# One written-out order for QKV, W1 and W2, 15 more warm-up transposes, and other staging rows for the last eight down tiles

## The chip, the cores and the metric

The kernel runs on one core of a Trainium2 chip. A core has five engines with a queue each: TensorE (PE) multiplies matrices, VectorE (DVE), ScalarE (ACT) and GpSimd (POOL) work on vectors, and SyncE (SP) issues DMAs. Each queue is worked off in order; an instruction that waits holds back everything behind it in its own queue and nothing in the others. The metric is device time in microseconds (us) of one execution; lower is better.

## The reference, cut to what matters

x has 2048 tokens of 576 channels. Two branches read the same layer-normed x, and their results are added to x.

```
xn  = layernorm(x)
out = x + A(xn) + B(xn)

A(x): qkv = layernorm-ed x @ wqkv          # 576 x 1728, 32 heads of 18
      windowed attention (8 keys, stride 2), then @ wo
B(x): h  = gelu(layernorm(x) @ w1)         # 576 x 576
      hs = shift(h) @ w2                   # four channel groups shifted by +1, -1, +2, -2 tokens
      x1 = x + hs
      x1 + gelu(layernorm(x1) @ w3) @ w4   # 576 x 4608 and 4608 x 576
```

## The kernel before

Everything is computed in single precision out of fp32r operands: each operand is split into a high part (a copy by ACT) and a low part (a subtraction by DVE), and a product is the sum of three matmuls (high x high, high x low, low x high). 576 rows are four blocks of 128 and a rest of 64; in PAIRS this gives 14 matmuls for an output tile. Tokens come in 16 tiles of 128 (t) and, transposed, in four blocks of 512 (b). Y holds the 16 token tiles in SBUF and rows of it serve as scratch in between.

The stages follow each other: QKV, W1, W2, then W3 and W4 with the attention beside them, then the output product with wo. The program is written in Python without a scheduler: the order in which the lines run is the order in each engine's queue.

**QKV** is written as a list. Each name of ORDER_Q (line 53) is a small function in T, and `for name in ORDER_Q.split(): T[name]()` runs them. The names that the prediction uses:

- x0 to x15 load a token tile, st its statistics (DVE, then a power by POOL), no its normalisation (DVE). ta copies its tail columns, tm and tt transpose main part and tail on PE into a PSUM tile of the pool psb (three of them), ch, cl, ct, cu cut the transposed tile into high and low parts (h and t on ACT, l and u on DVE).
- c0.0 to c3.2 load a column group of wqkv in three parts (two main parts, then the tail in four DMAs); wh, wl, wL, wt, wu, wU split it (h and t on ACT, l and u on DVE, L and U on POOL).
- u0.0 to u23.3 are the matmuls of 24 plain units of 14 matmuls each, in four pieces (6, 2, 4, 2); u0o copies the result out, u0s stores it to DRAM (qkvd). The pieces need, in this order: high parts and one low weight part, the other low weight part, the low part of x, the tails.
- zpad stores zeros in front of qkvd. pw does not exist before.
- From "mid" on, g6 to g15 are sums of seven products each on pairs of token tiles, fed by zg, zt, zp (a turned copy through DRAM), gp (reading it back), sx and ph, pl, pt, pu (sums and splits).
- w1m, w1t load w1, w1h and w1l split it; gz0.0 to gz0.5 load z, the turned x of a block of 512 tokens, and z0t, z0h0, z0h1 (ACT) and z0u, z0l0, z0l1 (DVE) split it.

In front of the list 24 transposes of the identity run on PE (line 454) into a tile of the pool psa.

**W1** is a loop over b and five tiles (lines 781 to 846). `mix_tile(b, m)` does 14 matmuls of 512 columns into a psb tile, two GELUs on ACT (into H[0][m] and into the scratch g32, one buffer) and one subtraction on DVE. `mix_rem(b)` does 9 matmuls for the remaining 64 columns, copies them to u (ACT), swaps halves of 16 partitions from u to v with eight DMAs on SP, and leaves an add, two GELUs and four placings into T4 (DVE) that the loop runs between later tiles. The loop also splits the next z block, loads and splits w2 in five pieces (`load_w2`, `split_w`; two buffers w2r), restores rows of Y (`back`) and loads the z block after the next. z blocks and the later blocks share a ring of two buffers.

**W2** is a loop over the 16 token tiles (lines 945 to 985): 28 matmuls of 288 columns, an addition into Y, statistics, and between them the loading of w3 and w4, and for the tiles 0 to 11 `n_turn`: two ACT passes, a DVE transpose into ST, and after every fourth tile four DMAs to xn; `get_n` reads a block back and `split_n` splits it.

**The last eight down tiles** (lines 1722 to 1736) finish W4. For the token tiles in YD the result is not added in SBUF: ACT copies it to a staging row of Y (`staging`, line 1124) and a DMA of POOL's queue adds it to yd in DRAM. A row can be used again once its DMA has read it. `load_y` brings the sums back to Y, and `split_x` splits the operands of the output product.

Of the kernel before, what the change touches and what calls it, by code (L numbers as in the profile page):

```python
# [17 lines left out]
NT = S // 128  # L18
# [41 lines left out]
u5.3 u4s u5o u5s sb0.2 wt0T3 sb0.3 st6 no6 u6.0 u6.1 u6.2 u6.3 u6o u6s u7.0 u8.0 u8.1 tt5 u7.1  # L60
u7.2 u7.3 cl4 u8.2 cu4 cl5 u8.3 wh0T3.1 st7 st9 u7o u9.0 st8 wh0T3.0 u9.1 u7s ct5 cu5 u9.2 u9.3
wh0T1.0 u8o u10.0 u9o wl1B11.0 u8s u9s u10.1 u10.2 u10.3 u10o wu0T3 u11.0 u11.1 u11.2 wh0T1.1
u11.3 wl0T3.0 u11o wl1B11.1 u11s u12.0 u12.1 wt0T1 wu1B11 u12.2 u12.3 u12o u13.0 u13.1 u13.2 u10s
no7 wl0T3.1 sc2 wl0T1.1 c3.0 c3.1 wl0T1.0 wu0T1 u14.0 u14.1 u13.3 sc6 u14.2 c3.2 u14.3 u12s early
zg6 zt6 zg7 u13o u15.0 u15.1 u15.2 u15.3 sc8 u13s zt7 zp3.2 wh1B12.0 wh1B12.1 zp3.1 wl1B12.0
wl1B12.1 u14o u16.0 u16.1 u14s wt1B12 zp3.0 zp3.3 sb1.0 wu1B12 sb1.1 sb1.2 sb1.3 u15o u16.2 u15s
wh1T1.0 u17.0 u16.3 u16o wl1T1.0 wh1T3.0 no8 u16s u17.1 u17.2 u18.0 u18.1 u17.3 u17o u18.2 u17s
u18.3 u18o u18s u19.0 u19.1 zg8 zt8 no9 zg9 zt9 u19.2 u19.3 u20.0 u20.1 u20.2 gp3.0 gp3.1 gp3.2
u19o wt1T3 gp3.3 gp3.4 wu1T3 gp3.5 sx3.0 u20.3 u21.0 u21.1 u20o u22.0 wh1T3.1 zp4.0 u21.2 zp4.3
zp4.1 zp4.2 u19s u21.3 pt3A12 pu3A12 u21o ph3A11 pt3A22 pt3A11 sx3.1 sx3.3 ph3S4 pu3A11 pu3A22  # L70
u22.1 u20s u22.2 u22.3 ph3S1 pl3A11 sx3.2 pt3S4 pu3S4 u23.0 u23.1 ph3A22 pl3A22 u23.2 ph3A12 u21s
ph3S3 pl3A12 pl3S4 x10 u23.3 gp4.0 gp4.1 pt3S3 pu3S3 pl3S3 wt1T1 wu1T1 pl3S1 pt3S1 pu3S1 wl1T3.0
wl1T3.1 wh1T1.1 wl1T1.1 st10 x11 st11 no10 gp4.2 gp4.3 gp4.4 u22o u22s gp4.5 sx4.0 u23o u23s mid
g6.1 g6c g7.1 g7c g6.5 g7.5 g6.2 ph4A11 pl4A11 g6o2 g6s2 sx4.2 ph4A12 aw0 g6.6 g6k5 g6k6 g7k5 g7.6
g7k6 g6.7 g6o7 sc10 g6s7 zg10 g6.3 x12 sx4.1 ph4S1 no11 zt10 zg11 g6o3 zt11 zg0 zp5.1 zp5.0 zp5.2
g6.4 g6o4 pt4A11 sc4 g7.7 g6s4 pl4S1 g7o7 zt0 pu4A11 pt4S1 zg1 zt1 pt4A12 pu4A12 sx4.3 g7.3 g7.2
g7o2 g7.4 g7o4 g8.1 g9.1 pu4S1 g8c g8.5 g7o3 g9.5 pt4A22 ph4A22 pu4A22 pt4S3 pl4A22 pl4A12 zg2
# [27 lines left out]
def fused_block(ctx, tc, x, wqkv, wo, w1, w2, w3, w4, out):  # L105
# [348 lines left out]
    warm = psa.tile([128, 512], F32, name="p1", tag="a")  # L454
    for i in range(24):
        pe.transpose(warm[:, :128], ident, ident)
# [197 lines left out]
    def back():  # L654
        for t in range(5):
            sp.dma_start(Y[:, t, :], ysp[t])

    for i in range(6):
        add(f"gz0.{i}", lambda i=i: get_z(0, ring_block(("z", 0)), i))
        add(f"gz1.{i}", lambda i=i: get_z(1, ring_block(("z", 1)), i))  # L660

    def split_z(what):
        xt = xring["z", 0]
# [15 lines left out]
    for w in ("t", "u", "h0", "l0", "h1", "l1"):  # L679
        add(f"z0{w}", split_z, w)  # L680
# [71 lines left out]
    T4 = mpool.tile([128, S + 4], F32R, name="T4")
    for g in range(4):
        for p in range(2):
            pool.memset(H[p][g][:, 0:2].bitcast(F32), 0.0)
            pool.memset(H[p][g][:, S + 2:S + 4].bitcast(F32), 0.0)
    pool.memset(T4[:, 0:4].bitcast(F32), 0.0)
    pool.memset(T4[:, S:S + 4].bitcast(F32), 0.0)
    mup = tc.tile_pool(name="mup", bufs=1, reuse_waits="tile")
    mupool = mup.__enter__()  # L760

    def load_w2(k):
        r = mupool.tile([128, D], F32, name="w2r", bufs=2)
# [17 lines left out]
    def mix_tile(b, m):  # L781
        xt = xring[("z", b)]
        ps = psb.tile([128, 2, 512], F32, name="ps", tag="b")[:, 0, :]
        for i, (a, w) in enumerate(PAIRS):
            pe.matmul(ps, W1[:, w, m * 128:(m + 1) * 128], xt[:, a, :],
                      start=i == 0, stop=i == len(PAIRS) - 1)
# [3 lines left out]
        act.activation(tokens(hi), turned_order(ps), AF.Gelu_apprx_tanh)  # L790
        act.activation(tokens(g32), turned_order(ps), AF.Gelu_apprx_tanh)
        dve.tensor_tensor(H[1][m][:, c:c + 512], g32, hi.bitcast(F32), op=ALU.subtract)

    def mix_rem(b):
        xt = xring[("z", b)]
        ps = psb.tile([128, 2, 512], F32, name="ps", tag="b")[:, 0, :]
        for a in range(9):
# [25 lines left out]
    for b in range(NB):  # L825
        for i, m in enumerate((0, 1, 2, 4, 3) if b < 3 else (4, 0, 1, 2, 3)):
# [8 lines left out]
            if (b, i) == (2, 0):  # L835
                back()
# [961 lines left out]
```

## Time and profile before

| what | us |
|---|---|
| median of 3 runs | 1262.52 |
| lowest, highest | 1260.89, 1262.6 |
| the profiled execution | 1261.03 |
| its span, first to last instruction | 1259.3 |

The profile shows one execution. 1.7 us of its 1261.03 lie around the span; sums below are made against the 1261.03. The profile has a page for the whole, and views: busy time in stretches of time, the timeline of an engine (start, length, line, operation, output <- input, and in brackets the idle time before it with what ended it), groups of instructions by line, and the chain of work that ended last. Between the instructions of a merged timeline row nothing idles that the profile shows. "PEclk" is the share of its clock that PE was granted.

### The profile page before, as it was taken

The numbers are of one execution on the slowest core, as the hardware profiler recorded it, in microseconds if no ns is written. First come the engines' busy times: TensorE is split into PE (matmuls) and PEld (weight loads), VectorE is DVE, ScalarE is ACT, GpSimd is POOL, SyncE is SP. The second block draws the span as 40 slices with busy tenths as digits, with TensorE's granted clock in tenths as the row PEclk, the third lists the DMA queues.
The fourth block names the chain that finished last, engine by engine and source line by source line (L and its number), as shares of the span: only waits on it lengthen the run. The fifth ranks groups of instructions, "written<-read, shape, count | busy, mean of one in ns | idle before, by whom it ended". The sixth has DMA issues, their size and how long they took to land.

```text
span 1259.3 us, 19957 instructions
## 1 busy us (share of the span) xinstructions
PE 1241.0 (99%) x7346; PEld 1141.6 (91%) x7346; DVE 932.4 (74%) x1182; ACT 759.8 (60%) x1234; POOL 278.7 (22%) x415
## 2 busy tenths in 40 slices
PE   8999999999999999999999999999999999999998
PEld 7999997799898999999899998999989999999898
DVE  6877645678458999997759998989989893554441
ACT  4556565526545545455867777776676776676620
POOL 5503100021222211212223232222122232222200
PEclk8999999999999999999999999999999999999999
DMA  8778993356888986769678898888968769899972
GB/s 221 178 181 200 196 236 111 116 155 177 207 226 183 222 159 145 158 137 246 124 174 188 196 186 210 180 167 212 258 114 186 141 128 199 182 210 232 261 241 78
DMA packets 221130, 230.50 MB, mean 183 GB/s; under 512 B 99544, under 2 KB 158136, under 8 KB 220904
## 3 DMA queue, kind: packets, MB, share of 16 engines
q1 hardware_dynamic: 188280, 162.43, 45.7%
q0 software_dynamic: 32752, 66.80, 32.8%
q8 instruction: 58, 0.95, 0.3%
q14 instruction: 40, 0.33, 0.1%
HBM read 130.76 MB, written 108.82 MB: 190 GB/s over the span
## 4 chain that ended last, share of the span: by engine, by line
PE 65%; DMA 3%; ACT 1%; DVE 1%; issue 1%; SPq 0%; POOL 0%; ACTq 0%; DVEq 0%; POOLq 0%
PE ps L1192 31%; PE cc L1456 19%; PE p L1156 10%; PE ps L252 4%; DMA w3st<-in_B_w_dram 1%; DMA yd<-ev 1%; DMA x1n<-xd 1%; DMA yd<-Y 1%; DVE xt L917 0%; SPq L1492 0%; PE p L1765 0%; DVE Y L1203 0%; ACT Y L1197 0%; ACT Y L1136 0%; DVE w3st L1289 0%
## 5 line engine op out<-in xcount | busy, mean ns | idle before, releaser
L1192 PEld LDWEIGHTS ps<-w,c 128*128 128x128 f32 x3456 | 477.8, 189 | 18.4 <-ACT Y L1197 2.9
L1192 PE MATMUL ps<-w,c 128*128 128x288 f32 x3456 | 487.8, 296 | 3.0 <-ACT Y L1197 1.6
L1198 POOL DMA_DIRECT2D yd<-Y x154 | 138.9, 905 | 369.8 <-ACT Y L1197 315.7
L1147 DVE TENSOR_TENSOR c<-Y,c 128x512 fp32r<-128x512 f32 x144 | 98.9, 687 | 89.2 <-ACT Y L1136 84.4
L1197 ACT COPY Y<-ps 128x576 f32<-128x576 f32 x154 | 97.9, 636 | 74.3 <-PE ps L1192 63.9
L1456 PE MATMUL cc<-xt,w3s 128*128 128x512 f32 (+1 forms) x504 | 127.2, 392 | 0.0
L1456 PEld LDWEIGHTS cc<-xt,w3s 128*128 128x128 f32 (+1 forms) x504 | 92.3, 188 | 17.3
L1200 ACT COPY Y<-ps 128x576 f32<-128x576 f32 x89 | 57.0, 640 | 59.4 <-PE ps L1192 58.0
L1067 DVE TENSOR_TENSOR po<-q,k 128x1152 f32<-128x1152 f32 (+1 forms) x48 | 84.2, 1755 | 0.8
L1070 DVE TENSOR_REDUCE L<-po 128x64 f32<-128x1152 f32 (+1 forms) x48 | 84.0, 1751 | 0.8
L1456 PE MATMUL cc<-x1n,w3a 128*128 128x512 f32 (+1 forms) x336 | 84.6, 392 | 0.0
L1135 ACT ACTIVATE c<-p 128x512 fp32r<-128x512 f32 x48 | 28.7, 598 | 86.3 <-PE p L1156 86.3
L1043 DVE TENSOR_TENSOR po<-v,L 128x1152 f32<-128x1152 f32 x56 | 75.4, 1354 | 0.9
L1466 DVE TENSOR_TENSOR Y<-cc,Y 128x512 f32<-128x512 f32 x49 | 33.7, 688 | 55.4 <-ACT Y L1462 49.7
L434 PE MATMUL p<-wb,xt 128*128 128x432 f32 (+1 forms) x336 | 69.8, 368 | 0.0
L1456 PEld LDWEIGHTS cc<-x1n,w3a 128*128 128x128 f32 (+1 forms) x336 | 60.4, 188 | 10.0
L434 PEld LDWEIGHTS p<-wb,xt 128*128 128x128 f32 (+1 forms) x336 | 64.7, 194 | 2.9
L1047 DVE TENSOR_TENSOR po<-po 128x1152 f32<-128x1152 f32 x49 | 66.4, 1355 | 0.9
L161 POOL TENSOR_TENSOR rs<-rs,mhalf 128x1 f32<-128x1 f32 x32 | 20.2, 632 | 183.8 <-DVE mv L164 106.4
L1173 ACT COPY ps<-Y 128x576 f32<-128x576 f32 x89 | 57.4, 645 | 3.1 <-DVE Y L1203 1.2
L701 PE MATMUL ca<-wb,xt 128*128 128x432 f32 (+1 forms) x280 | 58.4, 359 | 0.0
L701 PEld LDWEIGHTS ca<-wb,xt 128*128 128x128 f32 (+1 forms) x280 | 52.8, 189 | 2.4
(250 smaller groups left out, 2131.0 us busy)
## 6 DMA issues: line engine op xcount, KB each, us to landing
yd<-Y POOLq DMA_DIRECT2D x156, 288.0 KB, 6.2
Y<-in_B_w_dram SPq DMA_DIRECT2D x29, 576.0 KB, 5.7
w3st<-in_B_w_dram SPq DMA_DIRECT2D x56, 256.0 KB, 8.1
qkvd<-stg SPq DMA_DIRECT2D x44, 216.0 KB, 4.0
yd<-ev POOLq DMA_DIRECT2D x26, 288.0 KB, 6.8
w3st<-in_B_w_dram SPq DMA_DIRECT2D x92, 64.0 KB, 7.6
xd<-big SPq DMA_DIRECT2D x16, 320.0 KB, 6.9
Y<-in_A_x_dram SPq DMA_DIRECT2D x16, 288.0 KB, 4.9
```

The lines of the kernel that those rows point to most:

```text
L434: pe.matmul(ps[:, :QB], xo[:n, o + k, a, :], W[:n, w + k, v, :], start=i == 0, stop=i == len(PLAIN) - 1)
L701: pe.matmul(ps, form(g // 2, x, n, a), W[:n, OP[w], v, :], start=start and i == 0, stop=stop and i == len(HALVES) - 1, skip_group_check=True)
L1043: dve.tensor_tensor(dst, vv, Lf[:, :, w:w + 1].to_broadcast([128, TPP * GH, HD]), op=ALU.mult)
L1047: dve.tensor_tensor(o, o, dst, op=ALU.add)
L1067: dve.tensor_tensor(dst, qf[:, None, :].to_broadcast([128, n, TPP * GC]), win, op=ALU.mult)
L1070: dve.tensor_reduce(Lw[:, w:w + n, :], dst.rearrange("p w (x d) -> p w x d", d=HD), axis=AX.X, op=ALU.add)
L1147: dve.tensor_tensor(h[:, 1, :], g, h[:, 0, :].bitcast(F32), op=ALU.subtract)
L1156: pe.matmul(ps, W3[f][:, w, :], x1n[b][:, a, :], start=n == 0, stop=n == len(PAIRS) - 1)
L1192: pe.matmul(ps[:, k, :HF], h[:, col], w[:, p, k * HF:(k + 1) * HF], start=n == 0 and not seed, stop=n == len(seq) - 1, skip_group_check=True)
L1197: act.copy(e.rearrange("p (h c) -> p h c", h=2), ps[:, :, :HF])
L1198: pool.dma_start(yd[t], e, accum_op=ALU.add)
L1456: pe.matmul(ps, WX[w][:k, v, SLOT[w], :], area[sb][xk][:k, a, :], start=onto is None and i == 0, stop=last and i == len(HALVES) - 1, skip_ ...
```

## The change

**One list.** ORDER_Q grows from 747 to 1108 names. All names of before stay; 361 are new. Through QKV their order is another, and at the old list's end the list now goes on: "seam" closes the QKV pools and opens those of W1, "open3" those of W2. What the two loops did in whole tiles is cut into single operations with names:

- m00.0, m00.1: the first 8 and the last 6 matmuls of tile m of block b; the 14 are now sorted so that the first 8 need the blocks 0, 1 and 4 of z and the last 6 the blocks 2 and 3. mh and mg are its two GELUs, ml the subtraction; g32 has two buffers.
- r0, ro0, rs0.0 to rs0.7, rg0.0 to rg0.3, rp0.0 to rp0.3: the remainder, its copy, the eight swaps, add and GELUs and mask, and the placings.
- gz and z0t to z0l1 exist for all four blocks; vr, vh, vl load and split w2, bk restores a row of Y, hz zeroes a margin of H.
- w0.0, w0.1 are the two halves of a W2 tile, wy its addition, ws its statistics, yd its store; na and nt the two parts of `n_turn`, np a store to xn, gn and sn reading back and splitting; f3, h3, t3, v4, h4 load and split w3 and w4.

**Warm-up.** The identity transposes go to a tile of psb; pw0 to pw4 are three more each, so 15. Two stand in front of st0, three behind wl0B11.0.

**Last eight down tiles.** Rows 1 and 3 are loaded back after the eighth tile instead of the first, and are used as the first staging rows.

The core of the diff:

```diff
 ORDER_Q = """
-x0 st0 x1 st1 x2 c0.1 st2 no0 ta0 tm0 c0.0 c0.2 x3 c2.0 no1 tm1 no2 c2.1 c2.2 wh0B11.1 wL0B11.1
-wh0B11.0 wl0B11.0 ch0 tt0 ct0 tm2 x4 x5 ch1 st3 u0.0 u1.0 u1.1 cl1 u1.2 zpad cu0 cl0 no3 ta2
...
+x0 pw0 pw1 st0 x1 st1 no0 ta0 tm0 no1 tm1 x2 st2 c0.1 c0.0 zpad x3 c0.2 x4 c2.0 c2.1 c2.2 wh0B11.1
+wL0B11.1 ch0 no2 wh0B11.0 wl0B11.0 pw2 pw3 pw4 st3 tt0 cl0 ta2 tm2 ch1 cl1 x5 u0.0 ta1a u1.0 u1.1
+ct0 u0.2 tt1 wt0B11 ch2 ct1 no3 u1.2 cu0 tm3 ch3 wU0B11 u0.1 u0.3 u0o cu1 u1.3 u1o u0s cl2 tt2 ta3
...
+g15s3 seam hz5 hz1 m00.0 m01.0 m00.1 m02.0 m02.1 w1h3 w1h4 w1l4 vr0 mg00 vr1 m01.1 mh00 mh01 hz3
...
-    warm = psa.tile([128, 512], F32, name="p1", tag="a")
-    for i in range(24):
-        pe.transpose(warm[:, :128], ident, ident)
+    warm = psb.tile([128, 2, 512], F32, name="ps", tag="b")
+
+    def warm_up(n):
+        for _ in range(n):
+            pe.transpose(warm[:, 0, :128], ident, ident)
+
+    warm_up(24)
...
+    for i in range(16):
+        add(f"pw{i}", warm_up, 3)
...
+    def mix(b, m, n0, n1):
+        if n0 == 0:
+            mps[b, m] = psb.tile([128, 2, 512], F32, name="ps", tag="b")[:, 0, :]
+        xt, ps = xring["z", b], mps[b, m]
+        for i, (a, w) in list(enumerate(sorted(PAIRS, key=lambda s: s[0] % 5 in (2, 3))))[n0:n1]:
             pe.matmul(ps, W1[:, w, m * 128:(m + 1) * 128], xt[:, a, :],
                       start=i == 0, stop=i == len(PAIRS) - 1)
-        g32 = mupool.tile([128, 512], F32, name="g32", bufs=1)
+
+    def mix_leave(b, m, what):
         c = 2 + b * 512
         hi = H[0][m][:, c:c + 512]
...
+        elif what == "g":
+            g32[b, m] = mupool.tile([128, 512], F32, name="g32", bufs=2)
+            act.activation(tokens(g32[b, m]), turned_order(mps[b, m]), AF.Gelu_apprx_tanh)
+        else:
+            dve.tensor_tensor(H[1][m][:, c:c + 512], g32[b, m], hi.bitcast(F32), op=ALU.subtract)
...
+    def w2_tile(t, n0, n1):
+        if n0 == 0:
+            wps[t] = psb.tile([128, 2, 512], F32, name="ps", tag="b")
+        ps = wps[t]
...
+        for i, (a, b) in list(enumerate(PAIRS))[n0:n1]:
+            for h in range(2):
+                pe.matmul(ps[:, h, :HF], xs(a), W2[:, b, h * HF:(h + 1) * HF],
+                          start=i == 0, stop=i == len(PAIRS) - 1)
...
+    for name in ORDER_Q.split():
+        T[name]()
...
         if j == 0:
             low_part(h21, Z4)
-            load_y((1, 2, 3, 5))
-            EV[0] = (9, 11, 10, 15, 13)
+            load_y((2, 5))
+            rows = (1, 3, 13, 15, 9)
+            EV[0] = tuple(rows[(i - evc[0] - 1) % 5] for i in range(5))
...
+        if j == 7:
+            load_y((1, 3))
```

The order through W1, from the seam on, as far as the prediction follows it:

```
seam hz5 hz1 m00.0 m01.0 m00.1 m02.0 m02.1 w1h3 w1h4 w1l4 vr0 mg00 vr1 m01.1 mh00 mh01 hz3
mh02 ml00 mg01 mg02 r0 ro0 rs0.0 rs0.2 rs0.6 rs0.4 w1l3 m03.0 m03.1 gz2.4 gz2.5 z1h0 z1l0 z1t z1u
gz2.0 gz2.1 hz6 z1h1 z1l1 vh1 m10.0 m10.1 rs0.1 m11.0 hz8 m11.1 ml01 mg03 mh03 m12.0 rs0.3 m12.1
mh10 ml02 bk2 mg10 r1 vl1 vh0 mh11 vl0 ml03 mg11 ml11 bk1 hz4 mh12 ro1 vr2 m13.0 gz2.2 gz2.3 z2h0
ml10 mg12 m13.1 z2l0 z2t z2u hz0 t30 rs0.5 z2h1 m20.0
...
mg22 gz3.2 gz3.3 z3h0 z3l0 z3t z3u rs1.3 r2 m23.0 ro2 rs1.5 rs1.7 rs1.1 rg1.0 z3h1 vr4 rs2.4
m23.1 mh22 z3l1 r3 mg23 rs2.0 m30.0
...
w8.0 w8.1 np0.3 wy8 ws8 np0.2 w9.0 w9.1
```

More of the change, by code (lines that the diff above doesn't have):

```diff
@@ L60 @@
[L60 to L65, printed above, removed]
@@ new lines @@
+ml10 mg12 m13.1 z2l0 z2t z2u hz0 t30 rs0.5 z2h1 m20.0 m21.0 mh13 z2l1 m21.1 bk3 rs0.7 rg0.0 mg13
+ml13 vr3 rg0.1 bk0 rg0.2 rs1.4 rs1.0 ml12 rs1.2 vh3 m20.1 rg0.3 rp0.0 rp0.3 mh21 gz3.4 rp0.1 rs1.6
+vh2 vl2 mg20 mg21 mh20 ml20 rp0.2 gz3.5 gz3.0 gz3.1 ml21 m22.0 m22.1 mg22 gz3.2 gz3.3 z3h0 z3l0
+z3t z3u rs1.3 r2 m23.0 ro2 rs1.5 rs1.7 rs1.1 rg1.0 z3h1 vr4 rs2.4 m23.1 mh22 z3l1 r3 mg23 rs2.0
+m30.0 rs2.2 rg1.1 rg1.2 mh23 m31.0 rg1.3 rp1.2 rp1.1 rp1.3 vl3 rs2.6 rp1.0 ro3 rs3.0 rs3.4 rs3.6
+m31.1 mh31 m30.1 ml22 rs2.5 mg30 m32.0 mh30 m32.1 m33.0 ml30 m33.1 rs3.2 ml23 mg31 ml31 mg32 mh32
@@ L652, in fused_block, with split_z @@
         add(f"w1l{m}", split_w1, m, 1)
[L654 to L663, printed above, removed]
+    for b in range(NB):
+        for i in range(6):
+            add(f"gz{b}.{i}", lambda b=b, i=i: get_z(b, ring_block(("z", b)), i))
+    def split_z(b, what):
+        xt = xring["z", b]
         raw = xt.bitcast(F32)
@@ L779, in turned_order @@
         return blk.rearrange("p (b q t c) -> p t b q c", b=2, q=4, t=2)
[L781 to L784, printed above, removed]
+    mps, g32, uv = {}, {}, {}
+    def mix(b, m, n0, n1):
[3 more added lines that the diff above has]
+        for i, (a, w) in list(enumerate(sorted(PAIRS, key=lambda s: s[0] % 5 in (2, 3))))[n0:n1]:
@@ L796, in mix_rem @@
-    def mix_rem(b):
-        xt = xring[("z", b)]
-        ps = psb.tile([128, 2, 512], F32, name="ps", tag="b")[:, 0, :]
-        for a in range(9):
-            pe.matmul(ps, W1R[:, a if a < 5 else a - 5, :], xt[:, a, :], start=a == 0, stop=a == 8)
-        u = mupool.tile([128, 512], F32, name="u", bufs=2)
-        v = mupool.tile([128, 512], F32, name="v", bufs=2)
-        act.copy(tokens(u), turned_order(ps))
-        for q in range(0, 128, 32):
+        if what == "h":
+            act.activation(tokens(hi), turned_order(mps[b, m]), AF.Gelu_apprx_tanh)
+        elif what == "g":
+            g32[b, m] = mupool.tile([128, 512], F32, name="g32", bufs=2)
+            act.activation(tokens(g32[b, m]), turned_order(mps[b, m]), AF.Gelu_apprx_tanh)
+        else:
+            dve.tensor_tensor(H[1][m][:, c:c + 512], g32[b, m], hi.bitcast(F32), op=ALU.subtract)
@@ new lines, in rem, with rem_out, rem_swap @@
+    def rem(b):
+        ps = mps[b] = psb.tile([128, 2, 512], F32, name="ps", tag="b")[:, 0, :]
+        for a in range(9):
+            pe.matmul(ps, W1R[:, a if a < 5 else a - 5, :], xring["z", b][:, a, :],
+                      start=a == 0, stop=a == 8)
+    def rem_out(b):
+        uv[b] = [mupool.tile([128, 512], F32, name=n, bufs=2) for n in "uv"]
+        act.copy(tokens(uv[b][0]), turned_order(mps[b]))
+    def rem_swap(b, i):
+        u, v = uv[b]
+        q = 32 * (i // 2)
+        if i % 2 == 0:
@@ new lines, in fused_block @@
+    for b in range(NB):
+        for m in range(4):
+            add(f"m{b}{m}.0", mix, b, m, 0, 8)
+            add(f"m{b}{m}.1", mix, b, m, 8, 14)
+            for w in "hgl":
+                add(f"m{w}{b}{m}", mix_leave, b, m, w)
+        add(f"r{b}", rem, b)
+        add(f"ro{b}", rem_out, b)
+        for i in range(8):
+            add(f"rs{b}.{i}", rem_swap, b, i)
+        for i in range(4):
+            add(f"rg{b}.{i}", rem_gelu, b, i)
+            add(f"rp{b}.{i}", rem_place, b, i)
+    wp = nsp = nspool = None
@@ new lines, in get_n1 @@
+    def get_n1(b, part):
+        if part == 0:
+            x1n[b] = ring_block(("n", b))
+        get_n(b, x1n[b], part)
+    for f in range(2):
+        for i in range(2):
+            add(f"f3{f}.{i}", first_w3, f, i)
+            add(f"h3{f}.{i}", first_split, f, i)
+        add(f"t3{f}", turned_w3, f)
+        for i in range(3):
+            add(f"gn{f}.{i}", get_n1, f, i)
+        for w in "tuabcdef":
+            add(f"sn{f}{w}", split_n1, f, w)
+    for b in range(3):
+        for q in range(4):
+            add(f"np{b}.{q}", n_put, b, q)
@@ L986, in fused_block @@
+    add("v4", load_w4, 0)
+    for i in range(2):
+        add(f"h4{i}", split_w4, 0, i)
+    for name in ORDER_Q.split():
+        T[name]()
     nsp.__exit__(None, None, None)
```

330 lines of the change are left out of this document (183 added, 147 removed).

## The prediction

> **What bounds the kernel now.** I read the page first, then busy time by stage, then the PE timeline where PE has holes. The page:
>
> ```profile
> span 1259.3 us, 19957 instructions
> PE 1241.0 (99%) x7346; PEld 1141.6 (91%) x7346; DVE 932.4 (74%) x1182; ACT 759.8 (60%) x1234; POOL 278.7 (22%) x415
> ```
>
> PE is the bound, so an order can win only where PE stands still or runs slowly. Busy time by stage (stretch, length, then busy us of PE, PEld, DVE, ACT, POOL; clock, DMA share, GB/s) for QKV, W1 and W2:
>
> ```profile
> 25.00:181.20 156.20, 156.20 (x797) 148.95 (x795) 111.04 (x196) 87.23 (x169) 37.35 (x67) 1.00 0.84 199
> 181.20:247.00 65.80, 60.52 (x261) 48.52 (x261) 37.81 (x52) 37.97 (x62) 0.80 (x18) 1.00 0.50 138
> 247.00:306.50 59.50, 59.50 (x450) 59.46 (x450) 49.31 (x118) 22.92 (x36) 12.26 (x30) 1.00 0.53 155
> ```
>
> QKV from 25 us on, and W2, have no hole: there the new order can only lose. W1 has 5.3 us of holes. The rest lies before 25 us. First the PE timeline there, then the granted clock per microsecond (the figure before the DMA share):
>
> ```profile
> 1.38 5.38 PE L456 MATMUL p<-ident 128*128 128x128 f32 x24 [1.38 <-POOL ident masks.py:199]
> 8.64 1.15 PE L350 MATMUL ps<-ident,Y 128*128 128x128 f32 x8 [1.89 <-DVE Y L168]
> 11.67 0.66 PE L354 MATMUL ps<-ident,Y 128*128 128x128 f32 x2 [1.88 <-POOL wb L326]
> ...
> 22.34 0.41 PE L354 MATMUL ps<-ident,Y 128*128 128x128 f32 x2 [0.77 <-POOL rs L161]
> ...
> 24.16 0.60 PE L350 MATMUL ps<-ident,Y 128*128 128x128 f32 x4
> 24.52 6.53 PE L434 MATMUL p<-wb,xt 128*128 128x432 f32 x32
> 30.89 0.38 PE L354 MATMUL ps<-ident,Y 128*128 128x128 f32 x2
> ```
>
> ```profile
> 10.00:11.00 1.00, 0.00 (x0) 0.00 (x0) 0.00 (x0) 0.87 (x2) 1.00 (x1) 0.86 1.08 236
> 11.00:12.00 1.00, 0.33 (x2) 0.36 (x3) 0.93 (x1) 0.53 (x2) 0.59 (x1) 0.50 1.02 291
> ...
> 17.00:18.00 1.00, 1.00 (x6) 0.96 (x4) 1.00 (x2) 0.00 (x0) 0.19 (x1) 0.73 0.64 222
> ```
>
> Full-speed prices: 32 matmuls fill 24.52 to 30.89, so 0.199 us each; four transposes fill 24.16 to 24.52, so 0.09 each. By 24.52 the list of before has 36 matmuls (u0, u1, u2.0, u2.1) and 28 transposes (tm0 to tm4, tt0 to tt3) behind it: 7.2 + 2.5 = 9.7 us. PE stands as if it had begun at **14.8** and never stopped. Of that, 1.88 + 0.77 are holes; and the clock was at half from about 10.7 (0.86) to 17.5 (0.73), of which PE worked from 11.67: 5.9 us at half, 2.9 lost.
>
> **The change, part by part.**
>
> *Start.* It adds 6 transposes behind the 24 and 9 behind tm1, puts no0 and no1 before st2, ch0 before wh0B11.0, and the small zpad DMA and x3 before c0.2. The rows that time this:
>
> ```profile
> 2.75 0.93 POOL L452 MEMSET Y<- 16x1008 f32 x1
> 6.52 0.55 POOL L161 TENSOR_TENSOR rs<-rs,mhalf 128x1 f32<-128x1 f32 x1 [0.52 <-DVE rs L160]
> 8.01 1.71 DVE L168 TENSOR_SCALAR Y<-Y,mv,rs 128x576 f32<-128x576 f32 x3
> 8.04 0.91 ACT L323 CAST wb<-rawa 128x864 fp32r<-128x864 f32 x1 [6.01 <-DMA rawa<-in_A_wqkv_dram]
> 10.13 0.91 ACT L323 CAST wb<-rawa 128x864 fp32r<-128x864 f32 x1 [1.18 <-DMA rawa<-in_A_wqkv_dram]
> 10.95 0.58 ACT L553 CAST xt<-ps 128x512 fp32r<-128x512 f32 x1
> 11.07 1.43 DVE L326 TENSOR_TENSOR wb<-rawa,wb 128x864 fp32r<-128x864 f32 x1 [1.35 <-ACT wb L323]
> ...
> 12.83 0.82 DVE L158 BATCH_NORM_STATS2 bn<-Y 128x6 f32<-128x288 f32 x2 [0.32 <-DMA Y<-in_A_x_dram]
> ...
> 14.00 0.69 DVE L555 TENSOR_TENSOR xt<-ps,xt 128x512 fp32r<-128x512 f32 x1
> ```
>
> The second tile's 1/std ends at 7.07; no1 (a third of 1.71, 0.57) ends near 7.7, where today both norms wait for st2. Thirty warm-ups at 5.38/24 = 0.224 end at 8.1, tm0 and tm1 (1.15) at 9.3, nine more (1.15/8 each) at 10.6. These 15 stand in a hole: on PE's path they cost nothing, since u0.0 cannot begin before its weights. Without that hole they would cost 0.224 x 6 + 0.144 x 9 = 2.6. tt0 begins today 0.14 after ch0's end (10.95 + 0.58); ch0 now ends near 9.6, so tt0 follows the warm-ups. u0.0 needs wh0B11.0: no later than today's 11.04 if c0.0 still lands at 10.13; as early as 10.5 if taking c0.2 from beside it helps. Its fifth matmul needs wl0B11.0, 1.43 more: 11.9 to 12.5. By then 4 matmuls and 14 transposes (2.1 us) are done: PE stands as if begun at 9.8 to 10.4. Behind it DVE must bring st3 and cl0 in time: today st3 starts at 12.83 and cl0 or its like ends at 14.69, 1.9 later; from 12.5 on that is 14.4, and u0.2 comes 10 matmuls behind, at 14.5. I take 10.2: **-4.6**, with ends -1.5 (the clock falls anyway) and -5.6 (both holes and all 2.9 gone). The warm-up tile now takes a bank of psb that tm2 takes over: both are PE's, so nobody waits. The wait of zpad on the memset (until 3.68) holds x3 and c0.2 back by some 0.6 us on SP; c0.2 feeds only u0.3, and x3 only tm3, both after 15 us.
>
> [...]
>
> *W1.* The PE rows, then what ACT and DVE spend and wait for in this stage:
>
> ```profile
> 181.22 9.84 PE L785 MATMUL ps<-xt,W 128*128 128x512 f32 x42
> ...
> 212.14 2.12 PE L785 MATMUL ps<-xt,W 128*128 128x512 f32 x8 [1.14 <-ACT g L791]
> 215.49 8.00 PE L785 MATMUL ps<-xt,W 128*128 128x512 f32 x34 [1.23 <-DVE xt L225]
> ...
> 230.48 0.73 PE L800 MATMUL ps<-xt,W1R 128*128 128x512 f32 x2 [1.78 <-ACT g L791]
> ...
> 234.33 12.88 PE L785 MATMUL ps<-xt,W 128*128 128x512 f32 x56
> 247.05 3.34 PE L252 MATMUL ps<-W,h 128*128 128x288 f32 x24
> ```
>
> ```profile
> L791 ACT ACTIVATE g<-ps 128x512 f32<-128x512 f32 x15 | 8.9, 593 | 3.3 <-DVE h L792 3.3
> L224 ACT CAST xt<-xt 128x1024 fp32r<-128x1024 f32 x6 | 6.3, 1049 | 4.9 <-DMA xt<-zt 4.9
> L819 DVE SCALAR_TENSOR_TENSOR T<-v,sgn,u 32x512 fp32r<-32x512 f32 x12 | 8.9, 744 | 0.4
> ```
>
> Without stalls 56 matmuls fill 234.33 to 247.05, 0.227 each. The stage's 16 x 14 + 4 x 9 = 260 need 59.0; it took 247.05 - 181.22 = 65.8. So **6.8** is lost (5.3 shown idle, the rest refilling after each wait). The causes are in the second fence: one g32 buffer makes ACT wait for DVE (3.3), and the z loads, issued behind eight swaps on SP, reach ACT late (4.9). The change gives g32 two buffers, issues the main z rows before the swaps' second halves, and orders each tile's first 8 matmuls so that they need only the first half of z.
>
> Is something else late next? I add the durations up, from m00.0 at 0 (copies and GELUs 0.6, z1h0 1.05; z1l0 1.23 as in the last fence of this part). Block 1: r0 ends at 11.6; ro0 and z1h0 end by 13.5, z1l0 by 14.7; m10.0 is due at 14.75. Block 2: r1 ends at 26.3; ro1, z2h0, z2l0 by 29.4; m20.0 due at 29.5. Block 3: r3 needs the bank that mh22 frees; ACT passes mg22, z3h0, z3t, ro2, z3h1, mh22 from 39.2 to 44.2; r3 is due at 44.3. All three are met with at most 0.1 to spare. I allow 0.5 for them: **-6.3**, ends -6.8 and 0. SP issues the same loads; the queue risk is a rival below.
>
> *QKV after 25 us, and W2.* No term is removed. DVE in W2 rises from 49.3 of 59.5 us by the third remainder's adds and placings (4 x 0.744 and, an estimate, 1.2 for two passes of 512 columns: 4.2) to 53.5, in one queue with the bank-freeing adds; w9's bank is free only when wy6 is done, due to the tenth. In QKV DVE and ACT (111.0 and 87.2 of 156.2) cover the moves on average. I take **+0.8** for both together, ends 0 and 5.
>
> *Last 8 down tiles.* The chain view's DMA, then the timeline:
>
> ```profile
> 1178.47 6.90 DMA yd<-Y
> ```
>
> ```profile
> 1183.47 0.62 ACT L219 CAST x1n<-x1n 64x512 fp32r<-64x512 f32 x1
> 1185.44 0.64 ACT L1197 COPY Y<-ps 128x576 f32<-128x576 f32 x1 [1.35 <-PE ps L1192]
> 1185.98 1.05 ACT L224 CAST x1n<-x1n 128x1024 fp32r<-128x1024 f32 x1
> 1187.06 1.23 DVE L225 TENSOR_TENSOR x1n<-x1n 128x1024 fp32r<-128x1024 f32 x1 [2.47 <-ACT x1n L224]
> 1188.21 0.75 DVE L1203 TENSOR_TENSOR Y<-ps,Y 128x576 f32<-128x576 f32 x1
> 1189.01 6.64 PE L1192 MATMUL ps<-w,c 128*128 128x288 f32 x48 [1.03 <-DVE Y L1203]
> ```
>
> The eviction at 1185.44 really waits for the row whose DMA lands at 1185.37. With a fresh row it follows L219 at 1184.09; L224 ends at 1185.7, L225 at 1186.9, L1203 at 1187.65, so PE resumes 1.3 earlier: **-1.3**, ends 0 and -1.4 (L219's end). Rows 1 and 3 then come back only after j = 7, while PE works on the first output tiles, whose three banks let an addition wait, and cost nothing; without that cover up to 6.9, one such DMA.
>
> Sum, against the profiled execution's 1261.03 (span 1259.3 and 1.7 around it; the median of runs is 1.5 higher, which I leave to the range): 1261.03 - 4.6 - 6.3 + 0.8 - 1.3 = **1249.6**.
>
> **Rivals.** *The clock falls anyway.* After tm1 PE has only nine warm-ups until tt0; if their density is too thin, one fall of the size seen costs up to 6.8/2 = 3.4: 1253.0. For it: two 1.9 us holes sufficed today; against: the longest hole left is under 1 us. [...]
>
> *New holes in QKV or W2.* DVE at 90% in W2, or a pair's loads late at a DMA share of 0.84: 5 in the place of 0.8, 1253.8. For it: W2's tenth at w9. Against: both stages are whole today, with DVE and ACT below 85%.
>
> *W1 keeps its holes.* The joints miss and the stalls only move: 1249.6 + 6.3 = 1255.9. Against: each waiting term above has its cause removed.
>
> *Slower: SP blocks.* vr2 waits for vl0, and gz2.2, gz2.3 and the swaps stand behind it; lateness passes to z2 and, through the ring, to z3. If each of the two blocks comes L late, PE loses 2L; slower than before from L above 6.4, half of 1262.5 - 1249.6. Price at 8: 1249.6 + 16 = 1265.6. Against: in the sums above vl0 follows m10's GELUs, near 21, some 8 us before m20.0.
>
> **How the numbers follow.** Forecast 0.60 (own range 1247 to 1252), clock 0.10, new holes 0.17, W1 keeps its holes 0.07, SP 0.06 (half of it within 0.2%). 0.2%, 2.5 us, is about what a measurement of this kernel can tell from no change. Faster 0.94, same 0.03, slower 0.03. The range takes in the first three and lower ends: 1246.5 to 1255.
>
> **What would show it.** Right: clock at 1.00 from 10 to 18 us; u4.0 (13.6 us of work behind tm0's start) near 23.8; W1 (m00.0 to w0.0) in 59 to 60 us without PE waits on ACT g or DVE xt; the L1192 waits after the last product's second tile gone. Wrong: a clock of 0.50 before 20 us, PE holes between 25 and 176 us, or in W2 behind the adds into Y.

## The result, and the profile after

| | before | after |
|---|---|---|
| median of 9 runs each, side by side | 1262.6 | 1255.71 |
| lowest, highest | 1260.22, 1264.81 | 1252.06, 1258.41 |
| the profiled execution (span) | 1261.03 (1259.3) | 1258.14 (1256.3) |

The ratio is 0.9949, with a 95% interval of 0.9932 to 0.9965: faster by 6.9 us, about half of the 13.0 that separate the forecast, 1249.6, from before. The time lies 0.7 above the range. The profiled execution of after is one of its slowest. The page of after:

```profile
span 1256.3 us, 19980 instructions
PE 1241.3 (99%) x7361; PEld 1144.4 (91%) x7361; DVE 931.6 (74%) x1182; ACT 759.4 (60%) x1234; POOL 285.7 (23%) x415
```

PE is busy for as long as before, so the 3.0 us by which this execution is shorter are idle time. What a lower clock costs counts as busy here: the 18 matmuls from 12.43 on take 5.33 with no idle time shown between them, where the same 18 take 3.77 at a clock of 1.00 (the hole before tm2 filled). The PE timeline of after, QKV first, then the first rows of W1, W2 and W3:

```profile
9.35 0.38 PE L374 MATMUL ps<-ident,Y 128*128 128x128 f32 x2
12.04 0.63 PE L370 MATMUL ps<-ident,Y 128*128 128x128 f32 x4 [2.31 <-DVE Y L188]
12.43 5.33 PE L454 MATMUL p<-wb,xt 128*128 128x432 f32 x18
...
23.07 0.60 PE L370 MATMUL ps<-ident,Y 128*128 128x128 f32 x4
...
30.77 1.83 PE L454 MATMUL p<-wb,xt 96*128 96x432 f32 x8
35.79 0.44 PE L374 MATMUL ps<-ident,Y 128*128 128x128 f32 x2 [3.19 <-POOL Y L362]
...
184.37 9.72 PE L827 MATMUL ps<-xt,W 128*128 128x512 f32 x42
...
243.43 5.19 PE L1016 MATMUL ps<-W,h 128*128 128x288 f32 x38
...
302.83 12.88 PE L1270 MATMUL p<-xt,w3a 128*128 128x512 f32 x56
```

There are two new holes: 2.31 before tm2, 3.19 before tt5. W1 (184.37 to 243.43) has no wait left. Each hole is followed by a fall of the clock, as busy time by stretch shows (the clock is the figure before the DMA share):

```profile
12.00:14.00 2.00, 1.96 (x9) 1.88 (x10) 1.93 (x6) 0.00 (x0) 0.00 (x0) 0.71 1.06 385
14.00:16.00 2.00, 2.00 (x7) 1.84 (x7) 1.97 (x5) 1.34 (x3) 0.93 (x3) 0.50 1.07 218
36.00:38.00 2.00, 2.00 (x9) 1.89 (x8) 1.60 (x2) 1.30 (x3) 0.00 (x0) 0.68 0.00 0
38.00:40.00 2.00, 2.00 (x7) 1.84 (x7) 1.64 (x3) 0.30 (x1) 0.00 (x0) 0.50 0.46 111
```

What ended the holes stands in the timelines of DVE and POOL in after, first no2 and wL0B11.1, then the first and the last of the four passes of sb0 (long subtractions of weight rows, DVE) beside ta5 and the end of sc0 (seven small operations on the statistics of two token tiles, POOL):

```profile
9.64 2.25 DVE L188 TENSOR_SCALAR Y<-Y,mv,rs 128x576 f32<-128x576 f32 x1 [0.67 <-POOL rs L181]
...
29.34 1.51 DVE L353 TENSOR_TENSOR rawa<-rawb,rawa 128x1296 f32<-128x1296 f32 x1
...
33.97 1.51 DVE L353 TENSOR_TENSOR rawa<-rawa,rawb 128x1296 f32<-128x1296 f32 x1
```

```profile
9.58 2.01 POOL L346 TENSOR_TENSOR wb<-rawa,wb 128x864 fp32r<-128x864 f32 x1
...
28.45 1.28 POOL L314 TENSOR_TENSOR rs<-rs,mhalf 128x1 f32<-128x1 f32 x1
29.69 1.56 POOL L315 TENSOR_TENSOR mv<-rs,half 128x1 f32<-128x1 f32 x1
31.23 1.57 POOL L314 TENSOR_TENSOR rs<-rs,mhalf 128x1 f32<-128x1 f32 x1
32.77 1.57 POOL L315 TENSOR_TENSOR mv<-rs,half 128x1 f32<-128x1 f32 x1
34.30 1.43 POOL L362 COPY Y<-Y 128x256 f32<-128x256 f32 x1
```

no2 takes 2.25, where the prediction had 0.57 for no1 and no other time for no2: it starts beside a POOL operation of 2.01 and ends 0.30 after it. The last four operations of sc0, one column each, take 1.3 to 1.6 apiece; each ends 0.4 after an operation of DVE ends, so one runs per operation of DVE. ta5, on which tt5 waits, stands behind them.

The tail in after: PE, then the addition that releases it, SP's issues, and the copy that waits for the fourth block of the output product's operand:

```profile
1171.35 11.42 PE L1306 MATMUL ps<-w,c 128*128 128x288 f32 x84
1183.29 6.64 PE L1306 MATMUL ps<-w,c 128*128 128x288 f32 x48 [0.52 <-DVE Y L1317]
1189.77 15.07 PE L272 MATMUL ps<-Wo,x1n 128*128 128x288 f32 x112
1206.88 16.41 PE L272 MATMUL ps<-Wo,xt 128*128 128x288 f32 x112 [2.04 <-DVE Y L1876]
```

```profile
1206.07 0.76 DVE L1876 TENSOR_TENSOR Y<-ps,Y 128x576 f32<-128x576 f32 x1 [4.72 <-DMA Y<-yd]
```

```profile
1188.64 1.41 SPq L231 DMA_DIRECT2D xt<-xd  x2
1190.15 4.52 SPq L1834 DMA_DIRECT2D Y<-yd  x2
```

```profile
1203.95 0.62 ACT L238 CAST xt<-xt 64x512 fp32r<-64x512 f32 x1 [2.91 <-DMA xt<-xd]
```

The waits of L1192 (here L1306) are shorter, but a new one stands behind them: rows 1 and 3 are read back behind read_xo(3), whose data lands only near 1203.9, and the addition of the output product's second tile waits for row 1 until 1206.07. By then the three banks of psb are full, and PE stands still. Behind this hole the clock falls a third time (0.87, 0.50 and 0.77 in the three stretches of 2 us from 1206 on): the 112 matmuls there take 16.41, where the 112 in front of the hole take 15.07.

### The profile page after: what moved, and what is told of

It is laid out like the page before. It is cut to its first block, busy times and chain, and to the rows that moved or that the text cites. A ratio compares the mean times of both kernels' runs of the same rounds, so it can differ in the third digit from the quotient of the medians.

```text
span 1256.3 us, 19980 instructions
## 1 busy us (share of the span) xinstructions
PE 1241.3 (99%) x7361; PEld 1144.4 (91%) x7361; DVE 931.6 (74%) x1182; ACT 759.4 (60%) x1234; POOL 285.7 (23%) x415
## 4 chain that ended last, share of the span: by engine, by line
PE 61%; issue 4%; DMA 4%; DVE 1%; ACT 1%; POOL 1%; SPq 0%; POOLq 0%; ACTq 0%; DVEq 0%
PE ps L1306 29%; PE cc L1570 18%; PE p L1270 10%; PE ps L272 3%; DMA yd<-Y 1%; DMA Y<-yd 1%; POOL yd L1312 1%; DMA w3st<-in_B_w_dram 1%; DMA w3s<-w3st 0%; DVE xt L970 0%; PE p L1882 0%; ACT Y L1250 0%; SPq L231 0%; DVE Y L1317 0%; DVE w3st L1403 0%
## 5 line engine op out<-in xcount | busy, mean ns | idle before, releaser
L1306 PEld LDWEIGHTS ps<-w,c 128*128 128x128 f32 x3456 | 477.8, 189 | 16.7 <-ACT Y L1311 1.6
L1306 PE MATMUL ps<-w,c 128*128 128x288 f32 x3456 | 487.3, 296 | 1.7 <-ACT Y L1311 0.9
```

The lines of the kernel that those rows point to most:

```text
L1306: pe.matmul(ps[:, k, :HF], h[:, col], w[:, p, k * HF:(k + 1) * HF], start=n == 0 and not seed, stop=n == len(seq) - 1, skip_group_check=True)
```

## The experiments

Each kernel was measured beside the kernel before on the same chip, in three groups of four, with before at 1262.79, 1262.11 and 1264.31. Where the list is a line shorter, line numbers are one lower (L369 for L370). Differences are of medians. An estimate: one fall of the size seen (18 matmuls in 5.33 for 3.77, so 1.6 of 1256 us) costs 0.001 or more of the mean granted clock, so an execution with a mean of 1.000 had none of that size.

### sc0 out of ta5's way

```diff
-... st5 no5 sc0 u2s c1.1 u3s ta5 ... x7 cu5 u9.1 ...
+... st5 no5 u2s c1.1 u3s ta5 ... x7 cu5 sc0 u9.1 ...
```

> The changed kernel with one name of the list moved: sc0 (seven small POOL operations) from in front of ta5 to behind cu5, so that ta5 follows the statistics of its tile on POOL. Theory A (queue): tt5 waited 3.2 us at 32.6 because ta5 stood behind sc0, whose seven operations took 6.9 us beside DVE's long sb0 passes, and the clock fell once more after that hole. Then the hole is gone (under 0.5), no clock of 0.50 between 36 and 41 us, W1's first matmul 3 to 5 us earlier than 184.4, and the median 3 to 5 below the changed kernel's 1255.7. Theory B (lead): PE is simply ahead of tile 5, whose statistics come late; then the hole stays above 2 us, now behind the normalisation, and the median moves by less than 1.

1252.14 (1249.78 to 1254.85), ratio 0.991 [0.9888, 0.9931]. The timelines of POOL and PE:

```profile
27.99 0.40 POOL L361 COPY Y<-Y 128x256 f32<-128x256 f32 x1 [0.75 <-DVE Y L187]
```

```profile
32.22 0.38 PE L373 MATMUL ps<-ident,Y 128*128 128x128 f32 x2
```

ta5 takes 0.40 again and tt5 waits for nothing. The hole is made in POOL's queue, by sc0 standing ahead of ta5.

### wL0B11.1 off POOL

```diff
-... wh0B11.1 wL0B11.1 ch0 no2 wh0B11.0 wl0B11.0 pw2 ...
+... wh0B11.1 ch0 no2 wh0B11.0 wl0B11.0 wl0B11.1 pw2 ...
```

> The changed kernel with the first low weight part cut by DVE (wl0B11.1 behind wl0B11.0) and not by POOL (wL0B11.1). Theory A (shared access): no2 took 2.25 us in place of 0.57 because POOL's 2.0 us subtraction ran beside it; tm2 waited 2.3 us for it and the clock fell. Then no2 takes 0.6, tm2 starts near 10.4 in place of 12.04, and the hole before it is under 0.8; the clock stays at 1.00 until 20 us; the start is 1.6 earlier plus up to 1.6 of half clock: the median 2 to 3 below 1255.7, if what follows keeps up. Theory B: no2 is slow by itself or for its DMA; then it takes above 1.5 again and nothing moves.

1252.62 (1249.81 to 1255.03), ratio 0.9912 [0.9891, 0.9933]. DVE, then PE:

```profile
9.60 0.58 DVE L187 TENSOR_SCALAR Y<-Y,mv,rs 128x576 f32<-128x576 f32 x1 [0.67 <-POOL rs L180]
```

```profile
10.32 0.63 PE L369 MATMUL ps<-ident,Y 128*128 128x128 f32 x4 [0.64 <-DVE Y L187]
```

no2 is back at 0.58, and tm2 comes 1.7 earlier, though DVE has 1 us more to do. What opened the first hole is POOL's subtraction beside no2; 0.64 of the hole is left.

The clock isn't all that varies between executions. The profiled one, at 1255.03 the slowest of the six, has a clock of 1.000, and its PE waits 1.65 before tt5, 1.8 for an eviction in the down tiles and 1.7 for the late row.

### Rows 1 and 3 not staged

```diff
-            load_y((2, 5))
-            rows = (1, 3, 13, 15, 9)
+            load_y((1, 2))
+            rows = (5, 3, 13, 15, 9)
...
-            load_y((1, 3))
+            load_y((3, 5))
```

> The changed kernel with staging rows (5, 3, 13, 15, 9) for the last eight down tiles: rows 1 and 2 are loaded after the first tile, 3 and 5 after the eighth. Theory A (late row): the output product's addition of tile 1 waited until 1206.07 for row 1, whose load was issued last, behind the operands of the output product in the same queue, and PE lost 2.0 plus refilling. Then that wait is gone, evictions of the last tiles stay as early as in the changed kernel, and the median is 2 to 2.4 below 1255.7. Theory B: the additions are late for DVE's splits and not for the row; then a wait of 1 to 2 us stays there and the median moves by less than 0.7.

1250.74 (1250.26 to 1255.22), ratio 0.9905 [0.9882, 0.9928]. The wait is gone:

```profile
1199.90 15.10 PE L272 MATMUL ps<-Wo,xt 128*128 128x288 f32 x112
```

But 5 us is more than the wait of 2 can give: in five of these six executions the clock was 1.000. An edit of the last 100 us cannot reach the first 40, so this was run again, below.

### The old QKV list with everything else changed

```diff
-x0 pw0 pw1 st0 x1 st1 no0 ta0 tm0 no1 ... g15s3 seam hz5 hz1 m00.0 ...
+x0 st0 x1 st1 x2 c0.1 st2 no0 ta0 tm0 c0.0 ... w1h3 ... seam hz5 hz1 m00.0 ...
```

> The changed kernel with the QKV part of the old list in front of the new part from the seam on, and without the 15 warm-ups: W1, W2 and the last eight down tiles are those of the changed kernel. Theory A (the QKV order costs): W1's first matmul at 181.2 as before, not 184.4; W1 again 59.1 long without waits; the median 1262.6 - 6.8 (W1) + 0.6 (the end) = 1256.4, no more than 1 above the changed kernel, so that the new QKV order with its warm-ups brings nothing as it stands. Theory B: W1's gain needs the new QKV order, which brings w1 and z earlier; then W1 starts later than 182 or takes over 61 us, and the median is above 1258.

The four names of w1's splits that the old list already has are left out behind the seam. 1253.76 (1252.35 to 1256.53), ratio 0.9924 [0.9903, 0.9944]; the clock was 0.995 to 0.998 in all. W1 begins here:

```profile
180.41 1.65 PE L826 MATMUL ps<-xt,W 128*128 128x512 f32 x6
182.62 7.76 PE L826 MATMUL ps<-xt,W 128*128 128x512 f32 x33 [0.55 <-ACT W L671]
```

W1 keeps its gain (59.9 us, with one wait left), and W1 begins 4 us earlier than in after. The new QKV list with its warm-ups, as it stands, brings nothing: without it the median is 2.0 below that of after.

### After again, and after without the 15 warm-ups

> The changed kernel itself, on the same chip as the next three, so that they are compared with it. Theory A (its time is the new order's holes plus a clock that falls in some executions in the holes of the first 40 us): 1254 to 1257 as a median, executions with a granted clock of 1.000 near 1252.5, those at 0.997 near 1257.5. Rival (the first measurement was a disturbed draw): below 1251, no such split by clock.

1256.1 (1251.58 to 1257.55), ratio 0.9933 [0.9908, 0.9958]. Of the 17 executions of after in both measurements three had a clock of 1.000 (1251.58, 1252.06 and 1253.03) and one 0.999 (1254.01); the other 13, at 0.995 to 0.997, took 1255.12 to 1258.41. So two draws of one program differ by some 4 us, along with the clock.

```diff
-x0 pw0 pw1 st0 ... wh0B11.0 wl0B11.0 pw2 pw3 pw4 st3 ...
+x0 st0 ... wh0B11.0 wl0B11.0 st3 ...
```

> The changed kernel without the 15 warm-up transposes in its list. Theory A (they fill holes of the first 10 us that stand anyway, and through that keep the clock up): the product's start moves by under 0.5 us, but the clock falls in more executions, so the median is 1 to 3 us later than the changed kernel's. Rival (the clock follows the hole before tm2 and the one before tt5, not the warm-ups): within 1 us of it. Second rival (the warm-ups delay the transposes behind them): 0.5 us or more faster.

1257.13 (1256.34 to 1262.07), ratio 0.996 [0.9942, 0.9978]: 1.0 later, with overlapping intervals, and none of 12 executions above a clock of 0.997. This alone doesn't tell the theories apart.

### All three repairs, with and without the warm-ups

> All three repairs together: sc0 behind cu5, wl0B11.1 on VectorE, and rows 1 and 3 not staged in the last eight tiles. Theory A (three separate costs): from the changed kernel at full clock, 1252.1 to 1253.0, less 3.2 for tt5's hole, less about 2.0 for the late row, less 1 to 1.7 for the hole before tm2: 1245.5 to 1247.5 at full clock, no PE wait of 1 us or more in the first 180 us, first W1 product near 177.5. Rival (each removed wait shows the next: what was gained by one is the same time): 1249.5 to 1250.5, no better than the best of the three alone.

1248.28 (1247.18 to 1249.13), ratio 0.9874 [0.9845, 0.9902], clock 1.000 in all four: 7.8 faster than after on the same chip, and 1.3 below the forecast. PE:

```profile
10.23 0.63 PE L369 MATMUL ps<-ident,Y 128*128 128x128 f32 x4 [0.17 <-DVE Y L187]
...
14.56 1.06 PE L453 MATMUL p<-wb,xt 128*128 128x432 f32 x4 [0.50 <-DVE xt L580]
...
17.93 1.05 PE L453 MATMUL p<-wb,xt 96*128 96x432 f32 x4 [0.48 <-POOL wb L553]
...
21.66 0.60 PE L369 MATMUL ps<-ident,Y 128*128 128x128 f32 x4
...
31.02 0.38 PE L373 MATMUL ps<-ident,Y 128*128 128x128 f32 x2
...
177.99 9.72 PE L826 MATMUL ps<-xt,W 128*128 128x512 f32 x42
...
1197.87 15.10 PE L271 MATMUL ps<-Wo,xt 128*128 128x288 f32 x112
```

No hole of 1 us is left behind the wait for the identity. The expectation was 0.8 us too low. It counted 3.2 for the second hole; in the executions profiled so far that had not lost clock in front of it, the hole was 1.65 (wL0B11.1 off POOL, and rows not staged). That this is the whole reason isn't shown: a later one (the hole before tm2 filled) had 3.20.

> The three repairs without the 15 warm-up transposes. Theory A (the warm-ups matter only while holes stand beside them): within 0.7 us of the three repairs with them, clock 0.999 to 1.000 in most executions. Rival (they are what keeps the clock in the first 12 us): the clock falls in most executions and the median is 1.5 to 4 us later.

1249.7 (1248.93 to 1250.25), ratio 0.9885 [0.9859, 0.9911]: 1.4 later than with the warm-ups, where "within 0.7" was expected; the rival's lower end, 1.5, is nearer. These are five and four executions, whose ranges just touch (1248.93 to 1250.25, and 1247.18 to 1249.13). Busy time and clock, with the warm-ups (first fence) and without:

```profile
8.00:10.00 2.00, 1.72 (x15) 1.33 (x13) 1.27 (x5) 1.63 (x3) 0.55 (x1) 1.00 1.07 284
10.00:12.00 2.00, 1.79 (x10) 1.27 (x10) 1.37 (x3) 1.47 (x3) 0.00 (x0) 1.00 1.05 230
```

```profile
8.00:10.00 2.00, 0.66 (x6) 0.33 (x4) 1.27 (x5) 1.45 (x3) 0.55 (x1) 1.00 1.09 292
10.00:12.00 2.00, 1.91 (x9) 1.63 (x8) 1.17 (x3) 1.64 (x3) 0.00 (x0) 0.59 1.05 220
```

The warm-ups fill a wait of tt0 on ACT, and without them the clock falls in this execution: 0.59 from 10 to 12 us. In one of the five it was 1.000 all the same. Keeping the clock is what the prediction has them do, if for less than its 2.9; in after, the hole of 2.31 that no2 leaves behind them undid it (0.71 from 12 to 14 us).

### The repairs of the first 40 us alone

The first two edits together, the tail as changed.

> The repairs of the first 40 us (sc0 behind cu5, wl0B11.1 on VectorE), the tail as changed. Against the three repairs together this prices the late row with the clock at full speed. Theory A (row 1, queued behind the fourth block of o, is late by 1.5 to 2.3 us in every execution): 1249.8 to 1251, one PE wait of 1.5 to 2.3 us at the output product's second tile. Rival (the row is late only in executions whose front was held up): within 0.5 us of 1248.3, no wait of over 0.5 us there.

1250.69 (1247.97 to 1259.1), ratio 0.9897 [0.9865, 0.993]. At a clock of 1.000 the median of five is 1249.69, 1.4 above the three repairs. That is a rough price of the late row at best: the chip is another one (before: 1264.31 against 1262.11), and the five spread over 3.2. The profiled execution, at 1247.97 the fastest, shows the smaller form of it:

```profile
1197.42 15.18 PE L271 MATMUL ps<-Wo,xt 128*128 128x288 f32 x112 [0.85 <-DVE Y L1875]
```

The time is the one expected, the wait is smaller: over all the executions profiled with this tail the row is late by 0.4 to 2.0. What sets this isn't shown.

### The new staging rows alone

```diff
-            load_y((1, 2, 3, 5))
-            EV[0] = (9, 11, 10, 15, 13)
+            load_y((2, 5))
+            rows = (1, 3, 13, 15, 9)
+            EV[0] = tuple(rows[(i - evc[0] - 1) % 5] for i in range(5))
...
+        if j == 7:
+            load_y((1, 3))
```

> The kernel before with the changed staging rows of the last eight down tiles and nothing else. Theory A (evictions gain 1.5 us, the late row takes 2.0 back): within 1 us of the kernel before, 0 to 0.5 us slower, with a wait of 1.5 to 2.3 us at the output product's second tile in place of waits of VectorE in the down tiles. Rival (the prediction's own term): 1.3 us faster with no such wait.

1264.34 (1259.92 to 1268.7), ratio 0.9996 [0.9971, 1.0022]. The new wait stands in PE's timeline:

```profile
1214.07 11.11 PE L252 MATMUL ps<-Wo,xt 128*128 128x288 f32 x70 [1.75 <-DVE Y L1762]
```

By itself this part of the change is worth nothing that can be measured, though the interval, about 3 us to either side, doesn't exclude the predicted 1.3. Nor does this execution show the shorter evictions: its last stretch of down tiles takes 20.5 us (1176.75 to 1197.24) against 19.9 before, because an eviction is late and PE waits 1.51 for it. In ACT's queue it stands behind casts of wo (two of these wait 0.44 and 0.68 for their loads in after); that late loads hold it up here is read from this order and isn't shown.

### The rows once more

> The repair of the rows alone once more, on another draw of chip: it gained 5 us where its wait is 2 us, because the clock did not fall in five of six executions. Theory A (the staging rows cannot touch the first 40 us; the clock there is the chance of the execution and the chip): clock 0.995 to 0.998 in most executions and about 1254, 1.5 to 2.5 below the changed kernel's 1256. Rival (leaving the rows out does keep the clock): 1.000 in most executions again and 1250.5.

1255.18 (1249.81 to 1256.92), ratio 0.9908 [0.9879, 0.9937]; 8 of 12 executions had a clock of 0.997. The first run of this kernel had drawn the good clock; its 5 us are not the edit's. Among executions at 1.000 the two runs have medians of 1250.58 and 1251.53, and after has 1252.06: 0.5 to 1.5 for the rows. Whether the chip, another one, or chance made the difference between the runs isn't shown.

### The hole before tm2 filled

```diff
-... tt0 cl0 ta2 tm2 ch1 ...
+... tt0 cl0 ta2 pw5 pw6 pw7 pw8 pw9 tm2 ch1 ...
```

> The changed kernel with 15 more warm-up transposes in the hole before tm2. Theory A (the first fall of the clock, at about 13 us, follows TensorE's idle 2 us there): the clock stays at 1.00 from 10 to 20 us and the fourth block's transposes (tm4) come 1.2 to 1.8 us earlier, near 21.5; the hole before tt5 stays, so 1252.5 to 1255 as a median. Rival (the clock falls for what the product itself asks, or by chance): it falls at 12 to 16 us as before, 1256.

1253.72 (1251.33 to 1255.38), ratio 0.9909 [0.9879, 0.9939]. PE:

```profile
10.21 1.80 PE L477 MATMUL ps<-ident 128*128 128x128 f32 x15
12.07 0.65 PE L369 MATMUL ps<-ident,Y 128*128 128x128 f32 x4
12.48 3.77 PE L453 MATMUL p<-wb,xt 128*128 128x432 f32 x18
...
21.64 0.60 PE L369 MATMUL ps<-ident,Y 128*128 128x128 f32 x4
...
34.37 0.69 PE L373 MATMUL ps<-ident,Y 128*128 128x128 f32 x2 [3.20 <-POOL Y L361]
```

tm2 begins when it did, but the 18 matmuls behind it take 3.77 instead of 5.33, and tm4 comes 1.4 earlier. Of the nine executions only this one has a clock as low as 0.997; of after's 17, 13 have 0.997 or less. So PE's idling before tm2 brings the fall here, or makes it likely. And tm4 comes as early as with the three repairs (21.66), where tm2 itself is 1.8 earlier: here the late no2 costs by the clock, hardly by the wait. The second hole is still there, and behind it the clock is 0.50 from 34 to 40 us.

## Why the forecast was too low

The profiled execution is 8.5 us above the forecast. The term of QKV brought 4.3 of this, the start 2.7 and what follows W2 1.9, while W1 gave 0.5 more than was counted. Even the three executions of after that kept the clock, at 1251.58 to 1253.03, are 2.0 to 3.4 above it. Two of the prediction's own signs of being wrong came: a clock of 0.50 before 20 us, and a PE hole between 25 and 176 us. (The lower ends of its terms add up to 1247.2, not to 1246.5; the result lies at the other end.)

**Start, -4.6: wrong.** By the prediction's own measure, tm4 in after has 40 matmuls and 24 transposes behind it in the list (8.0 + 2.1 = 10.1 us); at 23.07 PE stands as if begun at 13.0. Before had 9.3 us behind it at 24.16, so 14.9: -1.9. The step that failed is "no1 (a third of 1.71, 0.57)" carried over to no2, which the text had end in time without looking at what POOL did beside it; with it fell "the longest hole left is under 1 us". In at least 13 of 17 executions the clock fell, so the rival "the clock falls anyway" (1253.0) came true, but in a hole it had not named. Repaired, tm4 comes at 21.66, as if begun at 11.6 (-3.3); the waits of 0.50 and 0.48 left there, on cl0 and on wU0B11, are 1.0 of the 1.3 still missing.

**QKV after 25 us, +0.8: wrong.** W1's first matmul comes 3.15 later than before (184.37 against 181.22), with a start 1.9 earlier: +5.05. The hole before tt5 is 3.19 of this, and the second fall (about 1.5, by the size of the first: 5.33 against 3.77 for the same 18 matmuls) nearly all the rest. The step that failed is "DVE and ACT (111.0 and 87.2 of 156.2) cover the moves on average": it looked at loads, not at queues, and left out POOL, which was busy for only 37 of these 156 us. The rival "new holes in QKV or W2" had the size, 5, with DVE's load or late DMAs as its cause; the cause was an order in POOL's queue. With the three repairs W1 begins at 177.99, 3.2 earlier than before: the term is then about 0.

**W1, -6.3: right.** 184.37 to 243.43 is 59.06 against 65.83: -6.8, with no wait on ACT g or DVE xt. The three joints of 0.1 held, so the allowance of 0.5 was not needed. The rivals "W1 keeps its holes" and "SP blocks" fell.

**W2: right.** 59.40 (243.43 to 302.83) against 59.40 (247.05 to 306.45).

**Last eight down tiles, -1.3: half right.** The last stretch of down tiles and the first row of the output product in before:

```profile
1175.61 9.75 PE L1192 MATMUL ps<-w,c 128*128 128x288 f32 x72
...
1195.50 15.07 PE L252 MATMUL ps<-Wo,x1n 128*128 128x288 f32 x112
```

From the start of this stretch (in after: 1171.35), the output product begins after 18.4 instead of 19.9 us: -1.5, near the -1.3 worked out. In seven of the nine executions profiled with this tail it is 18.4; in the other two (wL0B11.1 off POOL, and the new rows alone) 20.4 and 20.5, with PE waits of 1.78 and 1.51 for a late eviction on ACT. "Cost nothing" failed: the load of row 1 is queued behind read_xo(3) and is late by 2.04 here. The text had this price only as what the missing cover would cost, and did not look up which DMAs stand ahead on SP. (That read_xo(3) is what holds the row up is read from the order of issue and landing; no run moves it.)

Sum in the profiled executions, from differences: start -1.9, QKV +5.05, W1 -6.8, W3 and W4 -2.1 (302.83 to 1189.77 is 886.94, against 889.05; 1.5 of it in the last tiles), output product +2.7 (to the span's end 66.5, against 63.8; 2.04 is the wait and 1.3 the fall behind it, and the rows after that are 0.7 shorter than before, for which no run shows a reason): -3.0, the difference of the spans. The medians differ by more, since this execution of after is one of its slowest.

Together the three repairs bring 7.8. Singly, by medians on other chips against 1256.1, moving sc0 gave 4.0, wL0B11.1 3.5, and the rows 5.4 and then 0.9. These can't be added up, because each median also holds the chance that the clock falls. Which executions keep the clock wasn't settled: one kernel (rows not staged) drew a clock of 1.000 in five of six executions on one chip and in three of twelve on another.

## What to carry to other kernels

When an order is changed by hand, list for each moved operation what the *other* vector engine does at that moment: no2 took 0.58 beside an idle POOL and 2.25 beside its subtraction of 2.01. An average over a stage clears an engine's load, not its queue: POOL was busy for 37 of 156 us in the QKV of before, and the new order of its queue opened a hole of 3.19. Follow the small operations of the idlest engine; what waited on them here was PE, busy for 99% of the span. And price a load by what is queued ahead of it on its engine, up to landing, before it is called free: row 1 was, and PE waited 2.04.

## What was not expected of the hardware

DVE's and POOL's operations took longer beside each other. no2, 0.58 where POOL was idle (wL0B11.1 off POOL), took 2.25 in after and ended 0.30 after POOL's operation of 2.01. POOL's one-column operations, 0.55 in a row quoted in the prediction (L161), took 1.56 beside DVE's passes of 1.51, so one per pass; a pass of DVE took 1.58 where POOL was idle for most of it (rows not staged, first run). The hole before tt5 was 1.65 where three of sc0's four one-column operations took over 1 us (1.04 to 1.57; rows not staged, first run), and 3.19 where all four did (1.28 to 1.57; after). Why the two engines slow each other isn't shown.

At TensorE, holes of 1.7 to 2.3 us before tm2 cost up to another 1.6 through the clock, and not in each execution. Behind one of 1.72 before tm2 the next 18 matmuls took 3.79 (rows not staged, first run), behind one of 1.77 they took 5.34 (after again). The same program took 1251.6 or 1257.6.

The two DMAs of 768 KB that load one block of the output product's operand landed 15 us after their issue in after (1188.64 to 1203.9), and the wait for a row of 288 KB issued 1.5 later ended only at 1206.07. The median of the ten such row loads is 5.3.
